# Two first loads move from SyncE to ScalarE, and GpSimd gives up one of the last stores

## The chip, the cores and the metric

The kernel runs on one core of a Trainium2 chip. A core has TensorE (PE in the profile; its weight loads are PEld), VectorE (DVE), ScalarE (ACT), GpSimd (POOL) and SyncE (SP). SyncE, ScalarE and GpSimd can issue DMA transfers, which 16 DMA engines carry out; SPq, ACTq and POOLq in the profile are these engines' own instruction queues. The metric is the device time of one execution in microseconds (us). Before the change it is 488.51 us, the median of 3 runs (488.5 to 489.9).

## The reference

Linear attention with elu+1 as its feature map, followed by a mixture of four experts:

```python
phi(x) = where(x > 0, x, exp(x) - 1) + 1
kv  = einsum('bhsd,bhse->bhde', phi(k), v)          # 8 batches, 8 heads, 576 tokens, 64 wide
z   = sum(phi(k), axis=tokens)
x   = einsum('bhsd,bhde->bhse', phi(q), kv) / (phi(q) . z + 1e-6)
x   = x with the heads side by side                 # 4608 tokens x 512
p   = domain_probs / (sum(domain_probs) + 1e-9)     # 4608 x 4
out = sum over e of p[:, e] * (relu(x @ w1[e]) @ w2[e])   # w1: 512 x 1024, w2: 1024 x 512
```

Everything comes in and goes out as 32-bit floats; the products are made in 16 bit.

## The kernel before

**Tiles.** Of each batch's 576 tokens, 512 make one tile of the expert part (tiles 0 to 7); the 64 that are left of each of the 8 batches make tile 8. So there are nine tiles of 512 tokens and 36 pairs of tile and expert. Each pair has two layers: the first (lines 655 and 868 for the matmuls, 852, 879, 894, 901 and 922 for what follows them) and the second (lines 715 and 810, with line 706 adding the weighted result to the tile `acc`). From tile 1 on the two layers use sums and differences of blocks, so that seven block products do the work of eight. GpSimd makes sums of the hidden layer (lines 777 to 783).

**Order.** The order of the work is written out by hand. The long list `CFG["EARLY"]` names steps one after another; each name advances one step, which emits its instructions on whatever engines it uses. The rest follows by position numbers. Every engine and every DMA queue runs its instructions in the order in which they were emitted, and waits where data are missing.

**The start.** For batch 0 all of q, k and v is loaded ahead of everything else. A piece of q is 256 KB (`load_q`, line 548): 128 partitions x 4 heads x 2 tokens x 64. A piece of k or v is 288 KB (`load_kv`, line 540): two heads, 576 elements in each of 128 partitions. Steps `lq0` to `lq3`, `lk0` to `lk3` and `lv0` to `lv3` issue one piece each; the engine that issues is taken from the strings `LQ`, `LK` and `LV`, one letter for each piece (S SyncE, A ScalarE). `lpr0` loads the first probabilities, always on SyncE. The order on SyncE is

```
lq2 lq3 lq0 lk0 lk1 lpr0 lv0 lv1 lk2 lk3 lv3 lv2 lq1
```

so "the second piece of q" is `lq3` and "the first of k" is `lk0`. The transfers of SyncE and ScalarE together use eight completion counters in turn; the ninth and every later one first waits until the transfer eight places before it has landed.

What uses the pieces: ScalarE makes the exponential of a q piece (`qe`, line 581) and of a k piece (`ke`, line 563); ScalarE's table load stands before the first of them. VectorE or GpSimd makes the linear part (`ql`, line 584; `kl`, line 566), VectorE the minimum of both (`qm`, line 587; `km`, line 570). TensorE transposes q (`qT`, line 595) and multiplies k and v (`kv`, line 606). The v pieces are cast by GpSimd, VectorE or ScalarE (`vc`, line 573). The first work is that of `lq0`: `qe0 ql0 ql3 qm0`, and then `qT0`. Between these steps stand matmuls on zeros (`warm`, line 997), 14 of them before the first transposition.

GpSimd issues the weights of the experts and the pieces of batch 1 (lines 224, 227, 230, 297, 319). Its first weight pieces, `w100` to `w102`, stand in its queue behind its cast of `lv0`; a further cast, of `lv3`, stands between `w102` and `w103`. Of GpSimd's transfers at most eight are under way too.

**The end.** The last pair (tile 8, expert 3) makes its second layer in the order of products 1, 2, 5, 6, 7, 3, 4, each for two groups of 128 rows (i = 0 and 1). Products 2, 7, 3 and 4 complete a quarter of the result; VectorE adds it to `acc` (line 706), and `store` writes it out (line 693) in two transfers of 64 KB, one for each half of the partitions. Which engine issues which half is in the dictionary `by` of `layer2_product`; a pair (p, i) that is not in it goes as "SA", first half on SyncE and second half on ScalarE. At the end every engine drains, SyncE waits until the stores have landed, and all engines meet (line 1146).

Of the kernel before, what the change touches and what calls it, by code (L numbers as in the profile page):

```python
# [70 lines left out]
    "TSUM1": (3.76, 4.1, 6.3, 9.92),  # L71
    "PR": (-21.88, 47.0, 56.27, 39.85),
    "LATE": (4.0, 14.0, 16.0, 24.0),
    "LQ": 'SSSS',
    "LK": 'SSSS',
    "LV": 'SSSS',
    "KL": 'VVVV',
    "VC": 'PVAP',
# [6 lines left out]
    "WARM": (14, 3, 2, 1, 5),  # L85
    "BANK": {'qT0': 'py', 'qT1': 'b', 'nd00': 'py', 'nd00+': 'b', 'kv2': 'py', 'xT00': 'b', 'kv3': 'b', 'nd10+': 'b', 'L00': 'b', 'L10': 'py', 'nd01': 'b', 'xT01': 'py', 'nd11+': 'b', 'L20': 'e', 'L30': 'e', 'L01': 'e', 'L11': 'py', 'L21': 'py', 'L31': 'b', 'b1.qT3': 'py', 'b1.nd30': 'py', 'b1.nd21': 'b', 'b1.q1': 'b', 'b1.qT1': 'py', 'b1.nd01': 'py', 'b1.xT2': 'b', 'b1.nd11': 'py', 'b1.xT0': 'b'},
    "EARLY": (
# [36 lines left out]
def kernel(  # L124
# [556 lines left out]
    def new_py():  # L681
        return ppm.tile([P, Dm], FP32, tag="py", bufs=2, name="py")

    def store(j, ns, cols=slice(0, Dm), engs=(nc.sync, nc.scalar)):
        acc = accs[j, ns][:, cols]
        if j < B:
            nc.sync.dma_start(
                out=out_b[j, 0:SM].rearrange("(p c) d -> c p d", c=CM)[ns],
                in_=acc,
            )  # L690
        else:
            for u in range(2):
                engs[u].dma_start(  # L693
                    out=out_b[2 * ns + u, SM:S, cols],
                    in_=acc[u * HP : (u + 1) * HP],
                )

    def add_acc(j, e, ns, ps, ds, first):
        if (j, ns) not in accs:
            accs[j, ns] = pm.tile([P, Dm], FP32, tag="acc", bufs=NACC, name="acc")  # L700
        acc = accs[j, ns][:, ds]
        pscal = p_sb[:, j, ns, e : e + 1]
        if first:
            nc.scalar.activation(acc, ps, AF.Identity, scale=pscal)  # L704
        else:
            nc.vector.scalar_tensor_tensor(  # L706
                out=acc, in0=ps, scalar=pscal, in1=acc, op0=AO.mult, op1=AO.add
            )
# [76 lines left out]
    def layer2_product(j, e, hT, hss, p, i):  # L785


        if (j, e) == (NTILES - 1, E - 1):
            if p == 1:
                pys[j, e, i] = [ppm.tile([P, DH], FP32, tag=tag, bufs=2, name=f"p{tag}") for tag in ("b", "e")]  # L790
            run, side = pys[j, e, i]
        else:
            if p == 2:
                pys[j, e, i] = new_py()
            run, side = pys[j, e, i][:, 0:DH], pys[j, e, i][:, DH:Dm]
        ts = slice(i * P, (i + 1) * P)
        ts2 = slice(NH + i * P, NH + (i + 1) * P)
        w, tw = w2_sb[e], t2_sb[e]
        lo, hi = slice(0, FH), slice(FH, FC)
        ps, lhsT, rhs, first = {  # L800
            1: (run, lambda k: hT[k // 2][:, k % 2, 0, ts], w[:, lo, 0:DH], (j, e) == (NTILES - 1, E - 1)),
            2: (side, lambda k: hT[k // 2][:, k % 2, 1, ts], w[:, hi, 0:DH], True),
            5: (side, lambda k: hss[k // 2][0][:, k % 2, ts], tw[:, 0], True),
            6: (run, lambda k: hss[k // 2][1][:, k % 2, ts], tw[:, 1], False),
            7: (run, lambda k: hT[k // 2][:, k % 2, 0, ts2], w[:, lo, DH:Dm], False),
            3: (side, lambda k: hss[k // 2][3][:, k % 2, ts], w[:, hi, DH:Dm], False),
            4: (run, lambda k: hT[k // 2][:, k % 2, 1, ts2], tw[:, 2], False),
        }[p]
        for k in range(FH):
            nc.tensor.matmul(  # L810
                out=ps,
                lhsT=lhsT(k),
                rhs=rhs[:, k],
                start=first and k == 0,
                stop=k == FH - 1,
                skip_group_check=True,
            )
        yield
        c1, c2 = slice(0, DH), slice(DH, Dm)
        ns, ds, first = {  # L820
            2: (i, c1, True),
            5: (2 + i, c2, True),
            1: (i, c1, False),
            6: (i, c2, True),
            7: (2 + i, c2, False),
            3: (i, c2, False),
            4: (2 + i, c1, True),
        }[p]
        add_acc(j, e, ns, ps, ds, first and e == 0)
        if (j, e) == (NTILES - 1, E - 1):  # L830
            if p in (2, 3, 4, 7):
                yield
                by = {(7, 0): "SP", (7, 1): "AP", (3, 1): "PP"}.get((p, i), "SA")
                store(j, ns, ds, [on[x] for x in by])
        elif e == E - 1 and p in (3, 4):
            yield
            store(j, ns)
# [166 lines left out]
    with tc.manual_schedule(  # L1004
# [57 lines left out]
        for n, (j, e) in enumerate(units):  # L1062
            h, hss = [None, None], [[None] * 4, [None] * 4]
            at = base + 2 * NSLOT * n
            for d in range(2):
                put_block(at + d * NSLOT, j, e, d, h)
            at += 2 * NSLOT + LAG

            def hsum(d, i, hT=h, hss=hss):
                hidden_sum(hT[d], hss[d], i)  # L1070

            for d in range(2):
                for i in range(4):
                    put_at(at + HSUM[d][i], f"hs{j}{e}.{d}{i}", hsum, d, i)
            order = L2ORD
            if n == len(units) - 1:
                order, at = (1, 2, 5, 6, 7, 3, 4), at + NSLOT
            for m in range(14):
                put_at(at + L2AT[m], f"m{j}{e}.{order[m // 2]}{m % 2}", layer2_product, j, e, h, hss, order[m // 2], m % 2)
# [71 lines left out]
```

## Time and profile before

| | us |
|---|---|
| median of 3 runs | 488.51 |
| the profiled execution | 487.91 |
| its span, first to last instruction | 486.1 |
| TensorE busy | 475.0 |
| GpSimd busy | 358.8 |
| ScalarE busy | 332.4 |
| VectorE busy | 376.5 |

The span leaves out 1.8 us of the execution's time, before and after the instructions. The granted clock of TensorE was 0.997 of full speed. TensorE's busy time contains the matmuls on zeros. The 16 DMA engines are busy throughout the first 70 us (shares above 1 come from packets that overlap), and less after that.

Rows of the waits read: who waited, for whom, total us, number of times, longest. Rows of the timeline read: start and length in us, engine, line, operation, output and inputs, number of instructions, and in brackets the engine's idle time before it and what ended it. Rows of the transfers read: what, queue, number, size of each, median us from issue to landing.

### The profile page before, as it was taken

Reading aid. Unit: us, or ns where it says so; the run is one execution under the profiler, and the core shown is the slowest. Engines: PE = TensorE matmul, PEld = TensorE weight load, DVE = VectorE, ACT = ScalarE, POOL = GpSimd, SP = SyncE. Lnnn points to the kernel's source line nnn. Section 1 sums busy time; section 2 is a strip of 40 time slices with the busy share of each in tenths; the row PEclk is TensorE's granted clock in tenths of the full one; section 3 lists DMA queues with packets and bytes.
Section 4 is the critical chain, followed back from the end, with each engine's and each line's share of the span. In section 5 each row is a group of like instructions: output and inputs, shape, how many; then the busy total and the mean of one; then the engine's idle time right before and its main releaser. Section 6 shows DMA issues by size and latency. Waiting matters only on the chain.

```text
span 486.1 us, 12014 instructions
## 1 busy us (share of the span) xinstructions
PE 475.0 (98%) x4565; PEld 407.3 (84%) x4565; DVE 376.5 (77%) x794; ACT 332.4 (68%) x662; POOL 358.8 (74%) x344
## 2 busy tenths in 40 slices
PE   6999999999999999999999999999999999999995
PEld 2766766899889888998889888988898888888884
DVE  5678997987968895888679876988687756775685
ACT  4788979956895599649874888478944565446530
POOL 4665044689966986789777977697769877987775
PEclk9999999999999999999999999999999999999998
DMA  8999987533345254524552346322220020002003
GB/s 271 214 218 261 234 214 194 140 103 93 113 150 114 41 151 156 120 53 112 185 123 56 114 139 149 77 82 100 76 61 19 7 93 2 1 4 85 2 1 86
DMA packets 79897, 53.67 MB, mean 110 GB/s; under 512 B 45152, under 2 KB 72544, under 8 KB 79840
## 3 DMA queue, kind: packets, MB, share of 16 engines
q1 hardware_dynamic: 70432, 40.99, 30.7%
q0 software_dynamic: 8928, 11.54, 12.3%
q8 instruction: 35, 0.57, 0.5%
q10 hardware_dynamic: 480, 0.39, 0.3%
q14 instruction: 22, 0.18, 0.1%
HBM read 45.16 MB, written 9.44 MB: 112 GB/s over the span
## 4 chain that ended last, share of the span: by engine, by line
PE 88%; DMA 6%; POOL 3%; issue 1%; SPq 1%; DVE 0%; POOLq 0%; ACT 0%; DVEq 0%
PE py L810 38%; PE pb L868 24%; PE pe L868 18%; DMA w<-in_moe_w_dram 5%; PE py L715 4%; PE psum_nd L472 1%; DMA vraws<-in_v_dram 1%; PE psum_kv L444 1%; POOL w L227 1%; POOL hs L783 0%; POOL hs L779 0%; POOL w L230 0%; PE psum_nl L490 0%; POOL out_dram L693 0%; POOL vpos L573 0%
## 5 line engine op out<-in xcount | busy, mean ns | idle before, releaser
L706 DVE SCALAR_TENSOR_TENSOR acc<-py,p_sb,acc 128x256 f32<-128x256 f32 (+1 forms) x382 | 182.2, 488 | 42.8 <-PE py L810 39.2
L852 DVE CUSTOM_DVE_ANT_0 h<-pe,u 128x512 f16<-128x512 f32 x140 | 96.1, 688 | 44.9 <-PE pe L868 28.8
L868 PEld LDWEIGHTS <-w 128*128 128x128 f16 x1120 | 108.9, 98 | 16.1
L777 POOL TENSOR_TENSOR hs<-h 128x512 f16<-128x512 f16 x64 | 74.6, 1166 | 57.0 <-DVE h L852 51.0
L810 PEld LDWEIGHTS <-h 128*128 128x128 f16 x1024 | 99.6, 98 | 12.3 <-issue 0.9
L810 PE MATMUL py<-w,h 128*128 128x256 f16 x744 | 106.4, 273 | 0.6 <-ACT acc L704 0.5
L879 ACT COPY u<-pb 128x512 f32<-128x512 f32 x140 | 82.4, 590 | 29.7 <-PE pb L868 27.7
L779 POOL TENSOR_TENSOR hs<-hs,h 128x512 f16<-128x512 f16 x64 | 74.0, 1157 | 26.7 <-PE py L810 24.2
L868 PEld LDWEIGHTS <-s 128*128 128x128 f16 x840 | 81.2, 98 | 12.7 <-DVE s L747 0.9
L868 PE MATMUL pb<-tt,w 128*128 128x256 f16 x560 | 83.8, 273 | 0.0
L810 PEld LDWEIGHTS <-hs 128*128 128x128 f16 x768 | 74.5, 98 | 8.8 <-issue 0.2
L783 POOL TENSOR_TENSOR hs<-h,hs 128x512 f16<-128x512 f16 x64 | 74.1, 1159 | 0.8 <-POOL h L781 0.8
L781 POOL TENSOR_TENSOR h<-h 128x512 f16<-128x512 f16 x64 | 74.5, 1165 | 0.1
L810 PE MATMUL py<-t,hs 128*128 128x256 f16 x496 | 74.1, 273 | 0.0
L901 ACT ACTIVATE h<-pe 128x512 f16<-128x512 f32 x70 | 41.9, 599 | 41.4 <-PE pe L868 39.1
L894 ACT COPY pe<-pb 128x512 f32<-128x512 f32 x70 | 40.0, 572 | 41.5 <-PE pb L868 15.8
L922 ACT ACTIVATE h<-pb 128x512 f16<-128x512 f32 x70 | 41.8, 599 | 6.3 <-PE pb L868 6.2
L868 PE MATMUL pb<-tt,s 128*128 128x256 f16 x280 | 41.8, 273 | 0.4 <-DVE s L747 0.4
L868 PE MATMUL pe<-tt,s 128*128 128x256 f16 x280 | 42.0, 273 | 0.0
L868 PE MATMUL pe<-xT,s 128*128 128x256 f16 x248 | 37.1, 273 | 0.0
L868 PE MATMUL pb<-xT,w 128*128 128x256 f16 x248 | 37.1, 273 | 0.0
L868 PE MATMUL pe<-xT,w 128*128 128x256 f16 x248 | 37.0, 273 | 0.0
(133 smaller groups left out, 594.2 us busy)
## 6 DMA issues: line engine op xcount, KB each, us to landing
out_dram<-acc SPq DMA_DIRECT2D x32, 256.0 KB, 2.5
w<-in_moe_w_dram POOLq DMA_DIRECT2D x14, 512.0 KB, 10.4
rawb<-in_k_dram SPq DMA_DIRECT2D x24, 256.0 KB, 3.0
rawb<-in_q_dram SPq DMA_DIRECT2D x24, 256.0 KB, 2.6
rawb<-in_v_dram SPq DMA_DIRECT2D x24, 256.0 KB, 2.8
rawq<-in_q_dram SPq DMA_DIRECT2D x4, 256.0 KB, 4.1
w<-in_moe_w_dram POOLq DMA_DIRECT2D x4, 256.0 KB, 5.8
rawb<-in_k_dram POOLq DMA_DIRECT2D x4, 256.0 KB, 10.5
```

Source lines behind the costliest of these rows:

```text
L706: nc.vector.scalar_tensor_tensor(out=acc, in0=ps, scalar=pscal, in1=acc, op0=AO.mult, op1=AO.add)
L777: nc.gpsimd.tensor_tensor(out=hs[0], in0=a21, in1=a22, op=AO.add)
L779: nc.gpsimd.tensor_tensor(out=hs[1], in0=hs[0], in1=a11, op=AO.subtract)
L781: nc.gpsimd.tensor_tensor(out=a21, in0=a11, in1=a21, op=AO.subtract)
L783: nc.gpsimd.tensor_tensor(out=hs[3], in0=a12, in1=hs[1], op=AO.subtract)
L810: nc.tensor.matmul(out=ps, lhsT=lhsT(k), rhs=rhs[:, k], start=first and k == 0, stop=k == FH - 1, skip_group_check=True,)
L852: nc.vector._custom_dve(TENSOR_ADD_SAT, out=out, in0=ps, in1=u, s0=BIG, s1=0.0)
L868: nc.tensor.matmul(out=ps[:, kk], lhsT=lk(kc), rhs=rhs[:, kc], start=first and kk == 0 and kc == 0, stop=kc == 1, skip_group_check=True,)
L879: nc.scalar.copy(u, self.b)
L894: nc.scalar.copy(self.e5, self.b)
L901: nc.scalar.activation(self.h[:, :, 0, 0:NH], self.e5, AF.Relu)
L922: nc.scalar.activation(self.h[:, :, 1, 0:NH], self.b, AF.Relu)
```

## The change

```diff
-    "LQ": 'SSSS',
-    "LK": 'SSSS',
+    "LQ": 'SSSA',
+    "LK": 'ASSS',
...
-        "lq2 lq3 lq0 qe0 ql0 ql3 qm0 lk0 kl0 lk1 lpr0 ke0 km0 qe2 ...
+        "lq2 lq3 lq0 lk0 qe0 ql0 ql3 qm0 kl0 lk1 lpr0 ke0 km0 qe2 ...
...
-                by = {(7, 0): "SP", (7, 1): "AP", (3, 1): "PP"}.get((p, i), "SA")
+                by = {(7, 0): "PP", (7, 1): "PA"}.get((p, i), "SA")
```

`lq3` and `lk0` are issued by ScalarE. `lk0` stands earlier in the list, ahead of `qe0`, so that both issues are the first two instructions on ScalarE, before its table load; nothing else on ScalarE, VectorE, TensorE or GpSimd changes its place there. SyncE issues

```
lq2 lq0 lk1 lpr0 lv0 lv1 lk2 lk3 lv3 lv2 lq1
```

and the eight counters are used in the same turn as before.

The last stores change as follows (first half / second half):

| product, group | before | after |
|---|---|---|
| (2, 0), (2, 1) | SyncE / ScalarE | SyncE / ScalarE |
| (7, 0) | SyncE / GpSimd | GpSimd / GpSimd |
| (7, 1) | ScalarE / GpSimd | GpSimd / ScalarE |
| (3, 0) | SyncE / ScalarE | SyncE / ScalarE |
| (3, 1) | GpSimd / GpSimd | SyncE / ScalarE |
| (4, 0), (4, 1) | SyncE / ScalarE | SyncE / ScalarE |
| transfers of SyncE, ScalarE, GpSimd | 6, 6, 4 | 6, 7, 3 |

What is computed stays the same.

2 rows, old and new, of the table nl are left out of this document.

## The prediction

> **What bounds the kernel now.** I read the page first (engine shares, chain that ended last), then the waits of TensorE, then the first 14 us instruction by instruction, and last the final 8 us.
>
> ```profile
> PE 475.0 (98%) x4565; PEld 407.3 (84%) x4565; DVE 376.5 (77%) x794; ACT 332.4 (68%) x662; POOL 358.8 (74%) x344
> PE 88%; DMA 6%; POOL 3%; issue 1%; SPq 1%; DVE 0%; POOLq 0%; ACT 0%; DVEq 0%
> ```
>
> TensorE is busy 475.0 of 486.1 us. Only 11.1 us are idle, so the question is where these lie and which of them the change can reach. The waits of TensorE and those of the first 31 us (total, times, longest):
>
> ```profile
> PE psum_qT L595 <- DVE qp L587: 1.9, 2, 1.5
> PE py L715 <- DMA w<-in_moe_w_dram: 0.2, 1, 0.2
> ACT ee L581 <- DMA rawq<-in_q_dram: 4.8, 1, 4.8
> POOL vpos L573 <- DMA vraws<-in_v_dram: 3.6, 1, 3.6
> PE py L810 <- ACT acc L704: 0.5, 1, 0.5
> PE pb L868 <- DVE s L747: 0.4, 1, 0.4
> ```
>
> The last two rows are all that TensorE waits for between 30 and 475 us (0.9 us with the third). In the middle it is dense: what is won or lost before 30 us is carried to the end, unless the 0.2 us wait for weights at 30.5 us grows. The beginning is a chain of transfers:
>
> ```profile
> 0.74 1.28 ACT L581 ACT_TABLE_LOAD   x1 [0.74 <-PEq L1135]
> 0.74 1.56 SPq L548 DMA_DIRECT2D rawq<-in_q_dram  x3
> 2.34 0.98 SPq L540 DMA_DIRECT2D kraws<-in_k_dram  x2
> 1.19 5.31 PE L997 MATMUL warm_ps<-qz 128*128 128x512 f16 x14 [1.19 <-DVE qz L176]
> 6.81 0.63 ACT L581 ACTIVATE ee<-rawq 128x512 f16<-128x512 f32 x1 [4.79 <-DMA rawq<-in_q_dram]
> 7.68 0.68 ACT L563 ACTIVATE kexp<-kraws 128x576 f16<-128x576 f32 x1 [0.24 <-DMA kraws<-in_k_dram]
> 7.97 0.40 PE L595 MATMUL psum_qT<-identh,qp 128*128 128x128 f16 x4 [1.47 <-DVE qp L587]
> ```
>
> SyncE issues the three q pieces (second, third and first by name: lq2, lq3, lq0) at 0.74, 1.26 and 1.79 us, 0.53 us apart, then lk0 at 2.34. ScalarE sits idle for 4.79 us until lq0 has landed; exponential, minimum and then the first real TensorE work (7.97) follow. The filler matmuls end at 6.50, so 1.47 us of TensorE idle hang on lq0. From issue to landing, one row for each of lq2, lq3, lq0, lk0 and lk1 in that order:
>
> ```profile
> rawq<-in_q_dram SPq DMA_DIRECT2D x1, 256.0 KB, 2.9
> rawq<-in_q_dram SPq DMA_DIRECT2D x1, 256.0 KB, 3.1
> rawq<-in_q_dram SPq DMA_DIRECT2D x1, 256.0 KB, 5.0
> kraws<-in_k_dram SPq DMA_DIRECT2D x1, 288.0 KB, 5.3
> kraws<-in_k_dram SPq DMA_DIRECT2D x1, 288.0 KB, 5.5
> ```
>
> They land at 3.64, 4.36, 6.79, 7.64 and 8.39 us. The third needs 2 us longer than the two before it, and in that time the transfer engines are not full (columns: stretch, its length, busy time of PE, PEld, DVE, ACT and POOL, clock, DMA share, GB/s):
>
> ```profile
> 3.00:3.50 0.50, 0.50 (x3) 0.18 (x2) 0.00 (x0) 0.00 (x0) 0.00 (x0) 1.00 1.14 344
> 3.50:4.00 0.50, 0.50 (x3) 0.15 (x1) 0.00 (x0) 0.00 (x0) 0.26 (x1) 1.00 0.88 254
> 4.00:4.50 0.50, 0.50 (x2) 0.15 (x1) 0.00 (x0) 0.00 (x0) 0.50 (x1) 1.00 0.52 144
> 4.50:5.00 0.50, 0.50 (x2) 0.15 (x1) 0.00 (x0) 0.00 (x0) 0.50 (x1) 1.00 0.83 171
> 5.00:5.50 0.50, 0.50 (x3) 0.22 (x2) 0.00 (x0) 0.00 (x0) 0.50 (x1) 1.00 0.76 224
> 5.50:6.00 0.50, 0.50 (x4) 0.26 (x3) 0.00 (x0) 0.00 (x0) 0.17 (x1) 1.00 1.15 343
> 25.00:30.00 5.00, 5.00 (x42) 3.85 (x41) 3.05 (x6) 4.01 (x8) 2.41 (x4) 1.00 1.26 221
> ```
>
> Between 3.5 and 5.5 us the share falls from 1.14 to 0.52 and comes back. Against 1.15 the four stretches lack 0.27, 0.63, 0.32 and 0.39, times 0.5 us: 0.81 us of share, or 0.7 us at 1.15. From 5.5 us on the transfers are full, still at 1.26 before 30 us, where TensorE waits 0.2 us for a weight piece. So only this hole can bring the weights forward.
>
> **The change, part by part.**
>
> *Two loads leave SyncE.* ScalarE issues lq3 and lk0 itself, ahead of its table load: two issues of about 0.5 us (the rows above: 1.56 us for three, 0.98 for two). The table load then runs from about 1.77 to 3.05 instead of from 0.74 to 2.02. ScalarE's next instruction waits for lq0, which lands after 5 us: the 1.03 us are hidden by a 4.79 us wait and would cost only if lq0 landed before 3.05. SyncE loses two issues: lq0 moves from 1.79 to about 1.26, lk0 (now ScalarE's) from 2.34 to about 1.26, lk1 from 2.89 to 1.79, and probabilities and v pieces come about 1.06 earlier. SyncE's ninth and later transfers stand behind landings of the first ones:
>
> ```profile
> SPq L540 <- DMA rawq<-in_q_dram: 0.9, 1, 0.9
> ```
>
> This is lv3 behind lq0's landing; the next one waits for lk0 in the same way. They move with those landings, and with full transfers after 5.5 us they cost nothing.
>
> *What an earlier lq0 is worth.* Least: nothing, if the issue time is not what it waits for. Plain: 0.53 us, its earlier issue with the same 5.0 us behind it. Most: had lq0 landed one piece's time (lk0 to lk1: 0.75) after lq3's 4.36, it would have come at 5.1 instead of 6.79, 1.7 us earlier; TensorE's filler lets it use only 1.47 of that. The loss end: lq0 now shares the engines with lk0 and lands when lk0 did, 7.64, 0.85 later. I take 5.6, 1.2 earlier: two queues have pieces ready at 3.5 us where one ran dry, but 288 KB of lk0 run beside lq0, so it doesn't reach 5.1. What is late next: lk0 was 0.24 us late for ScalarE and comes about 2 us earlier; lk1 and lv0 gain too. After 6.81 us the work is exp, minimum, transposes and casts one behind another, which move along with lq0.
>
> *The weights.* GpSimd issues the first weight pieces behind its cast of lv0:
>
> ```profile
> 9.24 0.70 POOL L573 CAST vpos<-vraws 128x576 f16<-128x576 f32 x1 [3.57 <-DMA vraws<-in_v_dram]
> 9.89 2.44 POOL L227 DMA_DIRECT2D w<-in_moe_w_dram  x3
> ```
>
> An earlier lv0 starts them earlier; but the piece that TensorE waits for at 30.5 us comes only as much earlier as the transfers lost less in the hole: 0.7 us by the mean share, up to 1.7 by the landing of lq0 (a landing waits for the last part, and a mean share hides that). TensorE's own 1.2 lies between. Out at 30.5 us comes the smaller of the two: I take 1.05, about midway between 0.7 and 1.47, because 0.2 us of wait are there already. Head: -1.05 us, from -1.47 to +0.85. A rule stands against it: the Trainium skill ("DMA: Bandwidth & Descriptors", section "Issuing engines are not separate DMA queues") says that transfers started by several engines run on the same sixteen DMA engines and interleave, so that a second issuer saves only its sequencer's issue time. By that the head is worth at most the 0.53 us of issue, and nothing if a full pipe stands behind it; the trace shows that the pipe is not full just then, with a share of 0.52.
>
> *Last stores.* The last item's stores go out in halves. Before, SyncE, ScalarE and GpSimd had 6, 6 and 4; after, 6, 7 and 3. GpSimd keeps both halves of (7,0) and the first of (7,1); both halves of (3,1) leave it.
>
> ```profile
> 479.35 0.58 POOL L693 DMA_DIRECT2D out_dram<-acc  x1 [0.51 <-DVE acc L706]
> 481.18 0.53 POOL L693 DMA_DIRECT2D out_dram<-acc  x1
> 480.10 0.56 ACTq L693 DMA_DIRECT2D out_dram<-acc  x1
> 481.45 0.76 ACTq L693 DMA_DIRECT2D out_dram<-acc  x1
> 481.39 0.55 SPq L693 DMA_DIRECT2D out_dram<-acc  x1
> out_dram<-acc ACTq DMA_DIRECT2D x1, 64.0 KB, 2.9
> L1146 POOLq DRAIN  x3: 46/93/4275, 481.1 to 485.9; - x3
> L1146 SPq DRAIN  x3: 7/7/7, 484.6 to 485.6; - x3
> L1146 POOLq EVENT_SEMAPHORE  x4: 17/17/17, 485.4 to 486.0; - x4
> SPq L1146 <- PEq L1146: 1.3, 2, 0.8
> ```
>
> ScalarE's last store lands at 481.45 + 2.9 = 484.35, and SyncE is through at 484.6; then it waits 0.8 us more. What still runs is GpSimd's drain, 4.28 us long, to about 485.45. So GpSimd ends the kernel, 0.65 us before 486.1. After: its three issues start at 479.35, 479.92 and about 480.48, the last 0.70 earlier than 481.18; if the drain follows its own last store, it ends near 484.75. ScalarE has one store more and its queue is tight: 479.53, 480.10, then by 0.56 each 480.66, 481.22, 481.78, so its last store comes 0.33 later and lands at 484.68; SyncE would be through at 484.93. The later of the two, 484.93, plus 0.65 is 485.58: 0.5 us less. I take -0.45, since the same bytes leave in less time. Bounds: -0.70 (GpSimd's whole shift) and +0.33 (the drain does not depend on its own stores, and ScalarE's later landing is added).
>
> *Sum.* -1.05 - 0.45 = -1.5 us. The profiled execution took 487.91 (486.1 and 1.8 around it), 0.60 below the median of 488.51. So 486.4 against the profiled one and 487.0 against the median. A measurement here tells about 0.3%, 1.47 us, from no change; the forecast lies just beyond it.
>
> **Rivals.**
>
> *The hole stays.* What empties the transfers between 3.5 and 5.5 us may be common to both issuers, since all pieces end in the same engines. For it: lq0's issue took no longer than lq2's, so SyncE was not what held it, and an earlier issue wouldn't help. Against it: two pieces ran well, and the third starved, on one queue. Then lq0 lands where it did, the head is worth 0, and with the tail -0.45 the time is 488.06: within 0.3%.
>
> *The tail is not GpSimd's.* If the drain is of a fixed end or follows the last landing of all, the tail is +0.33 and not -0.45. Against it: SyncE was through 0.8 us earlier. With the head of -1.05: -0.7, 487.8, within 0.3%.
>
> *lk0 gets ahead of lq0 (slower).* On one queue lq0's bytes come before lk0's. On two they take turns, at 3.5 us, where the engines starve. If the hole stays and lk0 takes its share of what flows, lq0 lands with lk0, at 7.64 (+0.85), or as late as lk1 did, 8.39 (+1.6), if lk0's larger packets go first throughout. All of ScalarE's and VectorE's work stands behind lq0 and TensorE's wait of 1.47 us grows by as much. For it: lk0's landing already lagged ScalarE by only 0.24, so it needs no speed; against it: the hole is a lack of ready work, which a second queue adds. It is slower than before from a landing of lq0 after 6.79 + 0.45 = 7.24 on, and by over 0.3% after 8.7, or after 7.93 if the tail is +0.33 too. Time: 488.9 to 490.4; I put it at 490.1, with the later landing of the two and a tail worth nothing.
>
> **How the numbers follow.** Forecast with both parts: 0.52, its own range 486.2 to 487.5; of this 0.44 lies below 487.04 and 0.08 above. Tail not GpSimd's: 0.12, of which 0.01 is beyond 0.3%. Hole stays: 0.20, within. lk0 ahead: 0.16, of which 0.14 is beyond 0.3%. Faster 0.45, within 0.41, slower 0.14. The point is the likeliest case's, 487.0. The range runs from 486.2 (head -1.47, tail -0.70, to 0.1) over the second and third case to 489.2; above it lies most of the slower case, below it some 0.04.
>
> **What the profile after would show.** ScalarE: two issues before the table load, the load ending near 3.05. lq0: its exponential starts near 5.6 instead of 6.81, TensorE's first transposes near 6.75 instead of 7.97; the DMA share from 3.5 to 5.5 us stays above 1.0. At 30.5 us the wait for weights is between 0.2 and 0.6. Last: GpSimd's last store issued near 480.5 in the tail's own time, its drain no longer the last, SyncE's wait of 0.8 gone. I am wrong if the exponential starts at 6.8 or later, if the share still falls to 0.5, if the wait at 30.5 us swallows what was won, or if SyncE still waits 0.8 us for GpSimd.

## The result and the profile after

| | before | after |
|---|---|---|
| median | 489.31 us (6 runs, 488.5 to 489.9) | 487.03 us (6 runs, 486.35 to 487.39) |
| ratio | | 0.9962, 95% interval 0.995 to 0.9973 |
| profiled execution, its span | 487.91, 486.1 | 486.35, 484.6 |

The changed kernel is faster by 0.38% (0.27 to 0.5%); the quotient of the two medians, 0.9953, lies within the interval. The kernel before spreads more than it seemed: over 35 later executions it ran from 486.83 to 491.27 us with a median of 488.32, and against that median 487.03 would be 0.26% less. So the two profiled executions, 1.5 us apart, are compared stage by stage below, and a stage is called changed only if other runs show it too.

The timeline of the first 13 us after the change, on ScalarE, TensorE and GpSimd, and two later rows of TensorE:

```profile
1.88 1.28 ACT L581 ACT_TABLE_LOAD   x1 [1.88 <-issue]
6.21 0.63 ACT L581 ACTIVATE ee<-rawq 128x512 f16<-128x512 f32 x1 [3.05 <-DMA rawq<-in_q_dram]
7.37 0.40 PE L595 MATMUL psum_qT<-identh,qp 128*128 128x128 f16 x4 [1.30 <-DVE qp L587]
8.72 2.39 POOL L227 DMA_DIRECT2D w<-in_moe_w_dram  x3
12.54 0.22 PE L628 MATMUL psum_num<-kvz,qT 128*128 128x128 f16 x1 [0.78 <-DVE kvz L617]
16.75 0.22 PE L628 MATMUL psum_num<-kvz,qT 128*128 128x128 f16 x1 [0.19 <-ACT kvz L617]
30.00 1.03 PE L715 MATMUL py<-w,h 128*128 128x512 f16 x4
```

The two issues, at 0.75 and 1.27, stand before the table load, which ends at 3.16, as forecast. The first exponential starts at 6.21 instead of 6.81, the first transposition at 7.37 instead of 7.97: 0.60 earlier, where 1.2 was forecast. The first weights are asked for at 8.72 instead of 9.89. In the last three rows TensorE has less left, as the same three matmuls of before show:

```profile
12.91 0.22 PE L628 MATMUL psum_num<-kvz,qT 128*128 128x128 f16 x1 [0.31 <-DVE kvz L617]
16.91 0.22 PE L628 MATMUL psum_num<-kvz,qT 128*128 128x128 f16 x1
30.52 1.02 PE L715 MATMUL py<-w,h 128*128 128x512 f16 x4 [0.20 <-DMA w<-in_moe_w_dram]
```

It is 0.37 us ahead at the first of them, where its wait for VectorE grew from 0.31 to 0.78, and only 0.16 ahead at 17 us, where a wait for ScalarE is new. At 30.5 us it is 0.52 ahead, because there the kernel before waits for a weight piece. The stretches of time, one of the kernel before and then those of the changed kernel, with the columns of the prediction's (the last two: share of the transfer engines, GB/s):

```profile
2.50:3.00 0.50, 0.50 (x3) 0.23 (x2) 0.00 (x1) 0.00 (x0) 0.00 (x0) 1.00 1.10 333
```

```profile
2.50:3.00 0.50, 0.50 (x3) 0.22 (x2) 0.01 (x1) 0.50 (x1) 0.00 (x0) 1.00 0.51 153
...
5.00:5.50 0.50, 0.50 (x4) 0.23 (x3) 0.00 (x0) 0.00 (x0) 0.50 (x1) 1.00 1.01 364
```

The hole between 3.5 and 5.5 us is gone: the share is lowest in its last half microsecond, at 1.01. A new one has opened between 2.5 and 3 us, 0.51 instead of 1.10. Of TensorE's waits up to 475 us:

```profile
PE pb L868 <- DVE s L747: 0.2, 1, 0.2
```

The 0.2 us wait for a weight piece is no longer there, and the wait for `s` (sums of weight blocks, line 747), at 54.5 us before, fell from 0.4 to 0.2. Behind it TensorE is 0.67 ahead, and 0.70 stand at the end. The end is measured from VectorE's last addition (the timeline's last row of line 706, before first and then after):

```profile
480.32 0.92 DVE L706 SCALAR_TENSOR_TENSOR acc<-pb,p_sb,acc 128x256 f32<-128x256 f32 x2
```

```profile
479.62 0.92 DVE L706 SCALAR_TENSOR_TENSOR acc<-pb,p_sb,acc 128x256 f32<-128x256 f32 x2
478.65 1.64 POOL L693 DMA_DIRECT2D out_dram<-acc  x3 [0.51 <-DVE acc L706]
L1146 POOLq DRAIN  x3: 46/93/4192, 479.6 to 484.3; - x3
L1146 SPq DRAIN  x3: 7/7/7, 483.7 to 484.1; - x3
SPq L1146 <- PEq L1146: 0.7, 2, 0.5
```

The addition ends at 481.24 before and 480.54 after: the **head** brought 0.70. From there to the end of the span it is 4.86 before (486.1) and 4.06 after (484.6): the **tail** brought 0.80. GpSimd's drain is as long as it was (4.19 against 4.28) but starts with its earlier last store; SyncE is through with the landings at 483.7, GpSimd's drain ends at 483.8 (479.6 and 4.19), and SyncE's longest wait for the others is 0.5 instead of 0.8.

### The profile page after: what moved, and what is told of

Same layout as the page of the kernel before. It is cut to its first block, busy times and chain, and to the rows that moved or that the text cites. A ratio compares the mean times of both kernels' runs of the same rounds, so it can differ in the third digit from the quotient of the medians.

```text
span 484.6 us, 12013 instructions
## 1 busy us (share of the span) xinstructions
PE 474.4 (98%) x4565; PEld 407.2 (84%) x4565; DVE 377.3 (78%) x794; ACT 332.2 (69%) x662; POOL 358.3 (74%) x343
## 4 chain that ended last, share of the span: by engine, by line
PE 90%; DMA 5%; DVE 2%; ACT 2%; issue 0%; POOL 0%; SPq 0%; ACTq 0%; DVEq 0%
PE py L810 38%; PE pb L868 24%; PE pe L868 18%; PE py L715 4%; DMA w<-in_moe_w_dram 2%; PE ph L655 1%; PE psum_nd L472 1%; DMA rawq<-in_q_dram 1%; DMA rawb<-in_q_dram 1%; DMA out_dram<-acc 1%; PE psum_kv L444 1%; PE pb L810 1%; PE pe L810 1%; DVE acc L706 0%; PE psum_nl L490 0%
```

## The experiments

**The loads alone, and the stores alone.**

```diff
# loads alone: LQ, LK and the list as in the change
-                by = {(7, 0): "PP", (7, 1): "PA"}.get((p, i), "SA")
+                by = {(7, 0): "SP", (7, 1): "AP", (3, 1): "PP"}.get((p, i), "SA")
```

> The two loads on ScalarE, the last stores as before. Theory (the parts are independent; read from the two profiles, where the last addition on VectorE ends 0.70 us earlier and the rest of the span is 0.80 us shorter): the last addition on VectorE ends near 480.5 instead of 481.24, the stretch from there to the end of the span stays at 4.86 us, the time is 0.7 us (0.15%) lower. Rival (the head is worth the 1.05 us that was forecast and the profiled pair shows less of it by chance): 1.0 us or more lower. Rival (the loads gain nothing by themselves; the early start and the end of the span vary from run to run): no difference, and the hole in the transfers back at 3.5 to 5.5 us.

```diff
# stores alone: by as in the change
-    "LQ": 'SSSA',
-    "LK": 'ASSS',
+    "LQ": 'SSSS',
+    "LK": 'SSSS',
...
-        "lq2 lq3 lq0 lk0 qe0 ql0 ql3 qm0 kl0 lk1 lpr0 ke0 km0 qe2 ...
+        "lq2 lq3 lq0 qe0 ql0 ql3 qm0 lk0 kl0 lk1 lpr0 ke0 km0 qe2 ...
```

> The last stores changed, the loads as before. Theory: the beginning is that of the kernel before (first transposition at 7.97), the last addition ends near 481.2, and the stretch behind it is 4.1 us instead of 4.86: time 0.8 us (0.16%) lower, GpSimd's drain again 4.2 us long but begun 0.7 us or more earlier. Rival (ScalarE's seventh store ends the kernel): SyncE's last wait for a landing ends later than 484.6 and the time is 0.3 us lower at most. Rival (drain not tied to GpSimd's own stores): no difference.

The loads alone took 487.25 us (12 runs), ratio 0.9976 (0.9963 to 0.999). The stores alone took 487.53 (11 runs), ratio 0.9992 (0.9979 to 1.0006), which by itself does not tell them from no change. The product of the two is 0.9968, inside the interval of the whole change. Of the loads alone, VectorE's last additions and SyncE's wait for the other engines:

```profile
479.67 0.92 DVE L706 SCALAR_TENSOR_TENSOR acc<-pb,p_sb,acc 128x256 f32<-128x256 f32 x2
SPq L1146 <- PEq L1146: 1.3, 2, 0.8
```

Of the stores alone, ScalarE's first exponential and VectorE's last additions:

```profile
6.57 0.63 ACT L581 ACTIVATE ee<-rawq 128x512 f16<-128x512 f32 x1 [4.55 <-DMA rawq<-in_q_dram]
480.45 0.92 DVE L706 SCALAR_TENSOR_TENSOR acc<-pb,p_sb,acc 128x256 f32<-128x256 f32 x2
```

The loads alone end the addition at 480.59 and leave the stretch behind it as it was, 4.81 of a span of 485.4, with SyncE's 0.8 us wait. The stores alone end the addition at 481.37, 0.13 later than before, and shorten the stretch to 4.03. So head and tail are separate parts, 0.65 to 0.70 and 0.80 to 0.83 by these profiles. The tail is firm: the stretch is 4.79 to 4.86 us in the five profiled kernels with the stores of before and 3.99 to 4.13 in the four with the new ones. The size of the head is not: two more kernels below have the change's loads, and there the addition ends at 481.16 and 480.93, only 0.1 and 0.3 earlier than before. By time the loads alone are worth 1.07 us between the medians, and 0.5 to 1.8 by the interval of the ratio, so neither the 0.7 that I expected nor the rival of 1.0 or more is decided. The first row of the stores alone also says how far one profile can be trusted: its loads are those of before, and the exponential still starts 0.24 earlier. Against that execution the head's first step is worth 0.37, not 0.60.

**Each load alone.**

```diff
# the q piece alone (stores as before)
-    "LQ": 'SSSS',
+    "LQ": 'SSSA',
```

> Only lq3 is issued by ScalarE; lk0 stays on SyncE, the stores as before. Theory (what fills the hole is that lq0 and lk0 no longer stand third and fourth on one queue): lq0 is issued at 1.26 and comes second on SyncE's queue; its exponential starts between 5.2 and 6.2, the share from 3.5 to 5.5 us stays above 1.0. If the new hole from 2.5 to 3.0 us (share 0.51 with both loads moved) comes from ScalarE's table load, which then runs from 1.25 to 2.5 us instead of 1.88 to 3.16, it moves 0.6 us forward; if it comes from two queues starting together, it stays where it is. Rival (only the time of issue counts): exponential at 6.3, hole as before.

```diff
# the k piece alone (stores as before)
-    "LK": 'SSSS',
+    "LK": 'ASSS',
...
-        "lq2 lq3 lq0 qe0 ql0 ql3 qm0 lk0 kl0 lk1 lpr0 ke0 km0 qe2 ...
+        "lq2 lq3 lq0 lk0 qe0 ql0 ql3 qm0 kl0 lk1 lpr0 ke0 km0 qe2 ...
```

> Only lk0 is issued by ScalarE, as its first instruction at 0.74; lq2, lq3 and lq0 stay on SyncE in this order, the stores as before. Theory (the third q piece on one queue starves): lq0 is issued at 1.79 as before and has 288 KB of lk0 ahead of it, the share holds up between 3.5 and 5.5 us because lk0 fills the hole, and the exponential of lq0 starts at 6.8 or later, so the time is the same as before or up to 0.5 us longer. Rival (a second queue with any piece is enough): exponential at 6.2, time 0.5 us lower.

The q piece alone took 487.22 us (10 runs), ratio 0.9974 (0.9961 to 0.9987); the k piece alone 487.14 (10 runs), ratio 0.9979 (0.9968 to 0.9989). Neither differs measurably from both loads together. At lq0 they differ clearly. The q piece alone, in the timeline and in stretches:

```profile
1.27 1.28 ACT L581 ACT_TABLE_LOAD   x1 [1.27 <-PEq L1135]
5.40 0.63 ACT L581 ACTIVATE ee<-rawq 128x512 f16<-128x512 f32 x1 [2.84 <-DMA rawq<-in_q_dram]
480.39 0.92 DVE L706 SCALAR_TENSOR_TENSOR acc<-pb,p_sb,acc 128x256 f32<-128x256 f32 x2
2.50:3.00 0.50, 0.50 (x3) 0.22 (x2) 0.01 (x1) 0.06 (x1) 0.00 (x0) 1.00 0.52 153
9.27:12.68 3.41, 1.52 (x40) 1.05 (x35) 3.04 (x6) 2.10 (x7) 3.41 (x6) 1.00 1.14 317
12.00:13.00 1.00, 0.61 (x6) 0.40 (x6) 0.53 (x4) 1.00 (x2) 1.00 (x2) 0.84 1.24 203
13.00:14.00 1.00, 1.00 (x4) 0.32 (x3) 1.00 (x3) 0.07 (x1) 1.00 (x3) 0.50 1.24 207
...
16.00:17.00 1.00, 0.84 (x40) 0.66 (x36) 0.78 (x2) 0.99 (x4) 1.00 (x2) 0.96 1.25 215
```

lq0 is used at 5.40: with lk0 kept behind it on SyncE, it comes even before the forecast 5.6, and moving lk0 as well costs lq0 0.81 us (5.40 to 6.21). But all of it is lost again. VectorE's last addition ends at 481.31, no earlier than before. On the way the granted clock stands at 0.50 (the column before the last two): 0.84 on the mean of the 13th microsecond, 0.50 in the three after it and 0.96 in the next, which is 0.32 + 3 + 0.08 = 3.4 us at half clock. In the 3.41 us ahead of it TensorE was busy for 1.52, 0.45 of the time: it was ready earlier and waited 0.8 us for v and 1.0 for `kvz`, which had not come earlier by as much, and the filler stands in the order by count. This fits the Trainium skill ("TensorE: Matmul & The Clock Gate", section "Part 1: The HAM clock gate") in the two clock values and in a window of about 3.4 us; it speaks of idle windows, though, and here TensorE was busy 0.45 of the time.

The k piece alone, in the timeline and in one stretch:

```profile
0.74 1.57 SPq L548 DMA_DIRECT2D rawq<-in_q_dram  x3
6.06 0.63 ACT L581 ACTIVATE ee<-rawq 128x512 f16<-128x512 f32 x1 [3.56 <-DMA rawq<-in_q_dram]
2.50:3.00 0.50, 0.50 (x3) 0.23 (x2) 0.00 (x1) 0.00 (x1) 0.00 (x0) 1.00 0.73 242
```

Here lq0 is asked for at the same moment as before, last of three on SyncE, and still used 0.75 earlier (0.51 against the 6.57 above). My expectation for this kernel was wrong: either piece on a second queue fills the hole, and lq0 gains though lk0 runs beside it. That also bears on the rule the prediction weighed, the Trainium skill's "DMA: Bandwidth & Descriptors", section "Issuing engines are not separate DMA queues": here a second issuer brought lq0 0.51 to 0.75 us with no issue time saved for it, while the one queue had not filled the transfer engines (the share from 3.5 to 5.5 us is shown under the next experiment). In these executions the rule does not hold.

**Longer runs on one queue.** A q piece is read in runs of 512 bytes (2 tokens x 64 x 4 bytes). This kernel is the one before, with the pieces cut so that a run is 1 KB.

```diff
-                out=t,
-                in_=q[0, g * HG : (g + 1) * HG, 0:SM].rearrange("h (p c) d -> p h c d", c=CM)[
-                    :, :, 2 * hf : 2 * hf + 2
-                ],
+                out=t.rearrange("p (a h) c d -> p a (h c d)", a=2),
+                in_=q[0, 2 * i : 2 * i + 2, 0:SM].rearrange("h (p c) d -> p h (c d)", c=CM),
```

> The kernel before, all loads on SyncE, but each q piece of batch 0 is read as two heads of four tokens: the same 256 KB in 256 runs of 1 KB instead of 512 runs of 512 B. The values then stand in other places of the tile, so q is wrong in batch 0; the work and its order stay. Theory (the engines run dry between 3.5 and 5.5 us because the many short runs of the q pieces are handed to them more slowly than they move them): with half as many runs the share in that stretch stays above 1.0 and the exponential of lq0 starts between 5.0 and 5.7 us instead of 6.6 to 6.8. Rival (the third transfer in a row on one queue starves whatever its runs): the hole stays at 3.5 to 5.5 us and the exponential starts after 6.4.

It was executed once and took 488.83 us, beside 488.3 for the kernel before (9 runs). Its lines are numbered two lower. First the whole stretch in the kernel before, in the stores alone (the same loads) and in the k piece alone; then this kernel's, with its deepest half microsecond, its exponential and a wait of TensorE:

```profile
3.50:5.50 2.00, 2.00 (x7) 0.68 (x5) 0.00 (x0) 0.00 (x0) 1.76 (x1) 1.00 0.75 198
```

```profile
3.50:5.50 2.00, 2.00 (x7) 0.67 (x5) 0.00 (x0) 0.00 (x0) 1.85 (x1) 1.00 0.84 249
```

```profile
3.50:5.50 2.00, 2.00 (x10) 0.77 (x7) 0.00 (x0) 0.00 (x0) 0.98 (x1) 1.00 1.13 345
```

```profile
3.50:5.50 2.00, 2.00 (x7) 0.68 (x5) 0.00 (x0) 0.00 (x0) 1.93 (x1) 1.00 0.96 277
4.00:4.50 0.50, 0.50 (x2) 0.15 (x1) 0.00 (x0) 0.00 (x0) 0.50 (x1) 1.00 0.91 231
5.80 0.63 ACT L579 ACTIVATE ee<-rawq 128x512 f16<-128x512 f32 x1 [3.79 <-DMA rawq<-in_q_dram]
19.29 1.16 PE L653 MATMUL ph<-xT,w 128*128 128x256 f16 x9 [0.65 <-DMA w<-in_moe_w_dram]
```

The hole on one queue shrinks from a share of 0.52 (0.72 in the stores alone) to 0.91 at its deepest. In bytes the gain is smaller: 277 GB/s over the stretch, against 198 and 249 with short runs and 345 with a second queue. So short runs explain a part of the hole, as far as one execution can show; 1.0 isn't reached, and 5.80 is just outside what was expected. The end came no earlier all the same. At the matmul that the kernel before starts at 16.91 us, TensorE was 0.94 ahead; then it waited for weights, 0.6 and later 0.2 us, and further on 0.7 for ScalarE.

**GpSimd with one store less, and with the last one.**

```diff
# one store less (GpSimd issues two)
-                by = {(7, 0): "PP", (7, 1): "PA"}.get((p, i), "SA")
+                by = {(7, 0): "PP"}.get((p, i), "SA")
```

> The changed kernel, but GpSimd issues only the two halves of (7,0); both halves of (7,1) go to SyncE and ScalarE. Measure: the stretch from the end of VectorE's last addition to the end of the span, 4.86 us before and 4.06 after. Theory (the drain ends about 4.2 us after GpSimd's own last store, and SyncE's wait for the last landing stands right behind it): the drain ends 0.55 us earlier and is out of it; SyncE and ScalarE then have 7 and 7 and their last stores come 0.0 to 0.5 us later, so the stretch is 4.1 to 4.5 us, no better than 4.06, and SyncE no longer waits for GpSimd at the end. Rival (GpSimd's drain alone ends the kernel): the stretch falls to 3.5 us.

```diff
# the last one too (GpSimd issues four)
-                by = {(7, 0): "PP", (7, 1): "PA"}.get((p, i), "SA")
+                by = {(7, 0): "PP", (7, 1): "PA", (4, 1): "PA"}.get((p, i), "SA")
```

> The changed kernel, with GpSimd asking for half of the very last store too, so that its own last store comes after VectorE's last addition instead of one piece before it. If the 4.2 us of GpSimd's closing drain count from its own last store: that store is asked for about 0.1 to 0.2 us after the last addition ends, the drain ends some 4.9 us after the addition, and the stretch from the last addition's end to the end of the span is 4.9 to 5.2 us instead of 4.06. If the end was set by where the stores land, whoever asked for them, the stretch stays at 4.4 us or less. A single look: the stretch is what it is read by, not the time.

Each was executed once (487.05 and 487.92 us) and is read by the stretch behind the last addition. With one store less:

```profile
480.24 0.92 DVE L706 SCALAR_TENSOR_TENSOR acc<-pb,p_sb,acc 128x256 f32<-128x256 f32 x2
L1146 POOLq DRAIN  x3: 46/102/4021, 479.7 to 485.0; - x3
L1146 SPq DRAIN  x3: 7/7/7, 484.4 to 484.7; - x3
```

With the last store too:

```profile
480.01 0.92 DVE L706 SCALAR_TENSOR_TENSOR acc<-pb,p_sb,acc 128x256 f32<-128x256 f32 x2
481.23 0.53 POOL L693 DMA_DIRECT2D out_dram<-acc  x1 [0.55 <-DVE acc L706]
L1146 POOLq DRAIN  x3: 46/102/4147, 481.2 to 485.9; - x3
L1146 SPq DRAIN  x3: 7/7/7, 484.3 to 485.6; - x3
```

One store less brings nothing against 4.06, nearly as expected: 4.04 us from 481.16 to 485.2. GpSimd's drain is over near 483.7 (479.7 plus 4.02), and SyncE sees the last landing only at 484.4, so now the landings set the end. With the last store GpSimd's drain starts at 481.2 and the stretch is 5.17 (480.93 to 486.1), while SyncE is through with the landings at 484.3. So the drain of 4.0 to 4.3 us begins, within 0.2 us, with GpSimd's own last store in the four kernels whose rows are shown; the change put it just level with the landings.

**The q piece alone with the new stores, then with more filler.**

```diff
# with the new stores (to the changed kernel)
-    "LK": 'ASSS',
+    "LK": 'SSSS',
...
-        "lq2 lq3 lq0 lk0 qe0 ql0 ql3 qm0 kl0 lk1 ...
+        "lq2 lq3 lq0 qe0 ql0 ql3 qm0 lk0 kl0 lk1 ...
```

> Only lq3 on ScalarE and the last stores changed; lk0 stays on SyncE. Theory (with lq3 alone lq0 lands 0.8 us earlier than with both, but the work that starts earlier leaves TensorE so idle between 10 and 13 us that its clock is granted at one half for 3.4 us in most executions, which takes back more than was won): the granted clock over the execution is 0.993 to 0.997 in most runs, the profile shows a stretch at 0.50 near 12.7 to 16.1 us, and the time is that with lq3 alone less 0.8 us: a ratio of about 0.996, no better than the full change. Rival (the half clock in that one profile was chance): clock 0.998 to 1.0 and a ratio of 0.994 to 0.995.

```diff
# with 7 more matmuls on zeros as well
-    "WARM": (14, 3, 2, 1, 5),
+    "WARM": (14, 3, 2, 5, 5, 3),
...
-        "warm3 kv1 lk3 kv0 kv0 kl2 kv1 kl3 w102 kv1 nd01 ...
+        "warm3 kv1 lk3 kv0 kv0 kl2 kv1 kl3 w102 kv1 warm5 nd01 ...
```

> The same with seven more filler matmuls on zeros (0.21 us each at full clock): four ahead of the second product of k and v, where TensorE waits 0.84 us for a cast, and three ahead of the first numerators, where it waits 1.0 us. Theory (low use of TensorE brings the half clock): no stretch at 0.50 after 10 us, granted clock 0.997 or more in nearly all runs, and the time 0.5 to 1.2 us lower than without the fillers, ratio about 0.994. Rival (the half clock does not come from low use, or the fillers stand in the way of the work): the clock stays as without them, or the time is the same or up to 0.5 us longer.

They took 486.43 us, ratio 0.9958 (0.9943 to 0.9973), and 486.55, ratio 0.9963 (0.9949 to 0.9976), 5 runs each. The same stretch without and then with the additional filler, and of the latter VectorE's last additions:

```profile
14.00:15.00 1.00, 1.00 (x9) 0.72 (x8) 0.41 (x2) 0.03 (x1) 1.00 (x2) 0.50 1.25 206
```

```profile
14.00:15.00 1.00, 0.85 (x40) 0.68 (x38) 0.77 (x2) 1.00 (x4) 1.00 (x2) 1.00 1.21 200
479.19 0.92 DVE L706 SCALAR_TENSOR_TENSOR acc<-pb,p_sb,acc 128x256 f32<-128x256 f32 x2
```

The filler takes the half clock away, and in the profiled execution the last addition ends at 480.11, 0.43 before the changed kernel's. The medians do not follow: the gain of 0.5 to 1.2 us that I expected over the version without filler isn't there. The mean clocks of that version's five executions ran from 0.996 to 1.0, and only two of them lie in the 0.993 to 0.997 that I expected of most; probably not each of them lost the stretch. Also, the waits further on take back most of what the filler wins: the matmul of 16.91 us in the kernel before starts at 17.61 without it and at 16.07 with it, 1.54 apart, and at the last addition 0.46 of that is left. The three versions with the new stores (0.9962, 0.9958, 0.9963) are not told apart.

## Why the prediction was right, and where its steps were not

The time, 487.0 forecast and 487.03 measured, and the sum of -1.5 us, which is also the difference of the two spans, came out. That they agree so closely is luck. The 487.0 stands on a median of 488.51 for the kernel before, which became 489.31 over six executions and 488.32 over 35 later ones. And in the profiled pair the two terms did not come out: the head was forecast at -1.05 and measured -0.70, the tail at -0.45 and measured -0.80. The errors cancelled. By time, the loads and the stores alone are too close to the noise to size either term.

One sum of the prediction is misread: TensorE's waits from 30 to 475 us are 0.9 us without the 0.2 for weights, and 1.1 with it.

*Issues and table load.* Right: two issues ahead of the load, its end at 3.16, hidden by a wait of 3.05 that is left over.

*lq0 at 5.6.* Mis-sized: 6.21 where the changed kernel uses it. The step counted the hole between 3.5 and 5.5 us as filled, which it was, and took nothing for lk0's bytes before lq0 or for a new hole. The q piece alone shows lq0 at 5.40, so lk0 beside it costs 0.81. The third rival's mechanism was real, then, near its smaller price of 0.85, and on top of a gain that outweighed it. The new hole between 2.5 and 3 us is there with the q piece moved (0.51 with the k piece, 0.52 without it), and smaller (0.73) with the k piece alone; it is not the later table load, which ends at 2.55 in the q piece alone.

*What stands behind lq0 moves along.* Wrong: of 0.60 at 7.4 us 0.37 is left at 12.5 and 0.16 at 17. VectorE's next two linear parts of k took longer beside GpSimd's cast, which the change brought to the same time. The two kernels' rows, before and then after:

```profile
11.72 0.85 DVE L566 TENSOR_SCALAR kpos<-krawt 128x576 f16<-128x576 f32 x2
12.32 0.78 POOL L573 CAST vpos<-vrawt 128x576 f16<-128x576 f32 x1
```

```profile
10.89 1.33 DVE L566 TENSOR_SCALAR kpos<-krawt 128x576 f16<-128x576 f32 x2
11.08 0.83 POOL L573 CAST vpos<-vrawt 128x576 f16<-128x576 f32 x1
```

The same two parts take 1.31 us in the loads alone and in the k piece alone, and 0.85 in the stores alone. That one slows the other is argued from these rows, not tried.

*The weights.* Wrong in sign: the wait at 30.5 us was to be 0.2 to 0.6 and vanished. TensorE's own lead was only 0.16 there, while the weights were asked for 1.17 earlier; the forecast had TensorE outrun them and took the smaller of the two gains. What came out, 0.52, is TensorE's small lead and the wait that went. The other profiles say the same. The table gives by how many us TensorE starts the same matmul earlier than in the kernel before; the heads of its columns are that kernel's starting times, and the last matmul. The kernels with the q piece alone are left out, because half clock or filler stands in between.

| kernel | 7.97 | 16.91 | 30.52 | 54.50 | last |
|---|---|---|---|---|---|
| the change | 0.60 | 0.16 | 0.52 | 0.67 | 0.70 |
| loads alone | 0.61 | -0.13 | 0.23 | 0.78 | 0.65 |
| the change, one store less | 0.55 | -0.20 | 0.17 | 0.72 | 0.08 |
| the change, the last store too | 0.48 | -0.23 | 0.13 | 0.68 | 0.31 |
| k piece alone | 0.52 | -0.14 | 0.23 | 0.78 | 0.44 |
| stores alone | 0.24 | 0.31 | -0.30 | -0.14 | -0.13 |
| longer runs | 1.01 | 0.94 | 0.51 | -0.77 | -0.95 |

In the first five, `lk0` is on ScalarE. At 17 us nothing of their early lead is left that is clear of the spread between executions; at 54.5 us all five are 0.67 to 0.78 ahead. In between, none of them waits for a weight piece on TensorE, while the three kernels with all loads on SyncE do (0.2, 0.6 and 0.8 us). The wait for `s` at 54.5 us is one for weights too: VectorE itself waits for a piece before it makes `s`, 0.68 us in the kernel before, 0.53 after the change, and not at that place in the loads alone. GpSimd asks for the first weights at 8.38 to 8.72 us in the five and at 9.33 to 9.89 in the three. So the head comes from earlier weights and hardly from an earlier lq0. This is read from the traces; no run asks for the weights earlier and changes nothing else. Behind 54.5 us, TensorE's waits for ScalarE (`acc`, line 704) differ between executions and decide how much of the lead arrives.

*GpSimd's drain.* Right, and shown from both sides: it starts with GpSimd's own last store. That store started at 479.76 (the three end at 480.29, and the last takes 0.53) instead of 481.18, 1.42 earlier, of which 0.72 belong to the tail; 0.70 was forecast.

*ScalarE's last store.* Mis-sized twice. The step kept the 2.9 us to landing, had the store issued 0.33 later in the tail and so SyncE through 0.33 later. The last store after the change:

```profile
481.42 0.55 ACTq L693 DMA_DIRECT2D out_dram<-acc  x1
out_dram<-acc ACTq DMA_DIRECT2D x1, 64.0 KB, 2.2
```

Counted from the last addition it is issued after 0.88 us instead of 0.21, 0.67 later, and it lands 0.7 us quicker. By the same count SyncE is through after 3.2 us instead of 3.4. The whole 0.80 could therefore be had, instead of the 0.45 that was forecast with a landing after 2.9 us.

*The rivals.* The hole did not stay. The tail is GpSimd's. lk0's cost exists, but the sign held.

## What to carry to other kernels

Here one queue left the transfer engines partly idle, and either piece moved to a second queue brought the piece that was waited for earlier, even when that one stayed; but a transfer that runs beside it takes bytes from it. An early lead has to be followed along the whole run: here it was nearly gone at 17 us, and what reached the end came from weights that no longer made TensorE wait. A closing drain that counts from an engine's own last store is shortened by letting that engine stop first, and only down to where the other stores land. Filler that is counted, not timed, has to be counted again when the data come earlier.

## What was not expected of the hardware

- TensorE's granted clock fell to 0.50 for 3.4 us behind 3.41 us in which it was busy 0.45 of the time. One microsecond of little work does not do it: in the kernel before TensorE was busy 0.16 of the time from 11 to 12 us, and 1.99 of 3.41 us, 0.58, shortly before that, and the clock stayed at 1.00. Where between 0.45 and 0.58 the limit lies, or whether it is one of this kind, is open:

```profile
7.00:10.41 3.41, 1.99 (x23) 0.96 (x25) 3.06 (x8) 3.17 (x7) 1.17 (x2) 1.00 1.03 392
11.00:12.00 1.00, 0.16 (x9) 0.14 (x10) 1.00 (x3) 0.25 (x2) 1.00 (x2) 1.00 1.06 372
```

- A queue of 512-byte runs filled the transfer engines to a share of only 0.52 at its lowest between 3.5 and 5.5 us, and 0.72 in another kernel with the same loads; with 1 KB runs the lowest there was 0.91.
- With q pieces on two queues from the start the share is only 0.34 to 0.64 between 2.5 and 3 us, against 0.99 to 1.10 with all loads on one. Why is open.
- GpSimd's closing drain took 4.0 to 4.3 us whether it had issued two, three or four of the last stores.
